# A conformer block on one core: two query blocks moved to an earlier place in attention, and a feed-forward block moved in front of the last query block

## The chip, the cores and the metric

The kernel runs on one core of one Trainium2 chip. The metric is the device time of one execution in microseconds (us). Run times are compared between kernels that ran on the same chip in the same rounds. In the profile, PE is TensorE's matmuls, PEld its weight loads, ACT is ScalarE, DVE is VectorE, POOL is GpSimd, SP is the DMA queue's engine.

## The reference, cut to what matters

```python
B, T, D, K = (2, 4000, 512, 3); F = 4 * D
h = _layernorm(x);  x1 = x + 0.5 * (_silu(h @ w_ff1_a) @ w_ff1_b)
h = _layernorm(x1); q, k, v = h @ w_q, h @ w_k, h @ w_v
p = _softmax(jnp.einsum('btd,bsd->bts', q, k) * scale)
x2 = x1 + jnp.einsum('bts,bsd->btd', p, v) @ w_o
# [...] then a gated convolution over time, a second feed-forward, a last layer norm
```

The kernel folds `w_q` and `w_k` into one matrix M, so one projection of the queries ("query block", four of them for a chunk) is all that stands before the scores.

## The kernel before: the parts concerned

Tokens are cut into 16 chunks of 508 (4 tiles of 127), 8 for each batch. Attention goes over the chunks of queries (`g`), and within each over 32 key tiles (`kt`). Four PSUM banks S take scores, query blocks and other things in turn; four banks Y collect the values of a chunk. The values of a key tile run four tiles behind its scores (`LAG`): `self.lags` is a queue of matmul groups that wait their turn, and `pop(n)` issues the next n of them. The "seam" below is the place where the last values of one chunk end and the first of the next begin.

```python
def q_group(self, b, qc, dc):                       # one query block: 4 matmuls, one copy
    s, sl = qc % 2, 1 if b or qc else 0             # sl: slot with the transposed rows
    ps, b_ps = self.sbank()
    for cc in range(DC):
        self.mm(out, self.M[:, cc, dc*128:(dc+1)*128], self.lnT[sl][:, :, cc, lo:lo + W // TPC], ...)
    # dc odd: VectorE copies the bank to qT[s]; dc even: ScalarE does

def attention(self, old, hook, done):
    LAG = 4
    for g in range(NCK):
        # [...]
        for kt in range(KT):
            # scores: 4 matmuls  ->  ScalarE: exp  ->  VectorE: acc += P
            # [...]
            self.lags.append(values)                # 4 matmuls into the Y banks
            if g == 0 and kt < LAG:
                self.pop({0: old // 2, 1: old - old // 2}.get(kt, 0))
            elif len(self.lags) > LAG:
                self.pop(1)
            if g + 1 < NCK and 7 <= kt < 7 + TPC:
                self.fetch_queries((g + 1) // TCB, (g + 1) % TCB, kt - 7)
            if g + 1 < NCK and kt in (14, 16, 18, 20):
                self.q_group((g + 1) // TCB, (g + 1) % TCB, (kt - 14) // 2)
            # [...]
            hook(g, kt)                             # from g = 2 on: a convolution block at kt 3

def copy_o(self, g):                                # when a chunk's last values are issued
    for dc in range(DC):                            # (simplified to the usual chunk)
        self.away("DVE" if dc % 2 else "ACT", self.OT[:, dc, lo:hi], self.Yb[dc][:, lo:hi], ...)

# between feed-forward and attention:
for dc in range(DC):
    self.q_group(0, 0, dc)                          # two feed-forward blocks are still pending
```

The last values of chunk `g` are issued at tile 3 of chunk `g + 1`; `copy_o` then empties the Y banks, and the first values of chunk `g + 1` at tile 4 want them again. Slot 1 of `lnT` shares its upper half with `sT`, the transposed sums of the chunk that just ended.

Of the kernel before, what the change touches and what calls it, by code (L numbers as in the profile page):

```python
# [16 lines left out]
TPC = 4  # L17
CHUNK = TPC * TILE
N = B * T
TCB = -(-T // CHUNK)  # L20
NCK = B * TCB
# [6 lines left out]
DC = D // 128  # L28
# [7 lines left out]
def width(c):  # L36

    return CHUNK if c % TCB < TCB - 1 else T - (TCB - 1) * CHUNK
# [214 lines left out]
class Conformer:  # L253
# [604 lines left out]
                                           reads=b_o[lo:hi], writes=[Buf("out")]))  # L858


    def q_group(self, b, qc, dc):

        s, sl = qc % 2, 1 if b or qc else 0
        ps, b_ps = self.sbank()
        W = width(qc)
        out = ps[:, 0:W].rearrange("p (t k) -> p t k", t=TPC)
        lo = self.query_at(qc, 0)[1]
        for cc in range(DC):
            self.mm(out, self.M[:, cc, dc * 128:(dc + 1) * 128], self.lnT[sl][:, :, cc, lo:lo + W // TPC],
                    cc == 0, cc == DC - 1, [self.b_M] + self.b_lnT[sl], b_ps)  # L870
        if dc % 2:
            self.S.op("DVE", lambda e: e.tensor_copy(self.qT[s][:, dc, 0:W], ps[:, 0:W]),  # L872
                      reads=[b_ps], writes=[self.b_qT[s][dc]])
        else:
            self.act(self.qT[s][:, dc, 0:W], ps[:, 0:W], AF.Copy, [b_ps], [self.b_qT[s][dc]])
# [6 lines left out]
        return qc * CHUNK + ti * n - lo, lo  # L882

    def fetch_queries(self, b, qc, ti):
        sl = 1 if b or qc else 0
        src, rd = self.keys_at(b, self.query_at(qc, ti)[0])
        self.transpose(self.lnT[sl][:, ti], src, rd, [self.b_lnT[sl][ti]])

# [35 lines left out]
    def attention(self, old, hook, done):  # L924
        S = self.S
        LAG = 4
        for g in range(NCK):
            b, qc = divmod(g, TCB)
            s, W = qc % 2, width(g)
            if self.any_score:  # L930
                if qc == 0:
                    self.pop(len(self.lags))
                    if b:
                        for kt in range(KT):
                            self.key_tile(1, kt)
                self.row_max(qc)
            for kt in range(KT):
                kc, kj = divmod(kt, TPC)
                ps, b_ps = self.sbank()
                p = self.nxt("Pa", self.NP - 1) if self.any_score else self.nxt("P", self.NP)  # L940
                for cc in range(DC):
                    self.mm(ps[:, 0:W], self.hT[kc][:, kj, cc, :], self.qT[s][:, cc, 0:W],
                            cc == 0, cc == DC - 1 and not self.any_score,
                            [self.b_hT[kc][kj], self.b_qT[s][cc]], b_ps)
                if self.any_score:
                    self.mm(ps[:, 0:W], self.one3, self.m3[:, 0:W], False, True,
                            [self.b_one3] + self.b_m3, b_ps)
                self.act(self.P[p][:, 0:W], ps[:, 0:W], AF.Exp, [b_ps], [self.b_P[p]], scale=SCALE)
                if kt == 0:
                    S.op("DVE", lambda e, p=p: e.tensor_copy(self.acc[s][:, 0:W], self.P[p][:, 0:W]),  # L950
                         reads=[self.b_P[p]], writes=[self.b_acc[s]])
                else:
                    n = REST if kt == KT - 1 else 128
                    acc = self.acc[s][0:n, 0:W]
                    S.op("DVE", lambda e, p=p, n=n, acc=acc: e.tensor_tensor(  # L955
                        out=acc, in0=acc, in1=self.P[p][0:n, 0:W], op=ALU.add),
                        reads=[self.b_P[p], self.b_acc[s]], writes=[self.b_acc[s]])

                if kt == KT - 1:
                    self.split_sums(g)  # L960
                    if g < NCK - 1:
                        self.sums_by_query(s)

                def values(kt=kt, p=p, g=g, W=W):
                    for dc in range(DC):

                        r = slice(dc * REST, (dc + 1) * REST) if kt == KT - 1 else slice(0, 128)
                        self.mm(self.Yb[dc][:, 0:W], self.h[kt][r, dc * 128:(dc + 1) * 128], self.P[p][r, 0:W],
                                kt == 0, kt == KT - 1, [self.b_h[kt], self.b_P[p]], self.b_Y[dc],
                                inc=kt == KT - 1 or dc == DC - 1,  # L970
                                **({"tile_position": (dc * REST, 0)} if kt == KT - 1 else {}))
                    if kt == KT - 1:
                        self.finish_queries(g, done)

                self.lags.append(values)
                if g == 0 and kt < LAG:
                    self.pop({0: old // 2, 1: old - old // 2}.get(kt, 0))
                elif len(self.lags) > LAG:
                    self.pop(1)
                if g + 1 < NCK and 7 <= kt < 7 + TPC:  # L980
                    self.fetch_queries((g + 1) // TCB, (g + 1) % TCB, kt - 7)
                if g + 1 < NCK and kt in (14, 16, 18, 20):
                    self.q_group((g + 1) // TCB, (g + 1) % TCB, (kt - 14) // 2)
                if not self.any_score and TCB - 1 <= g <= TCB:

                    at = (g - TCB + 1) * KT + kt
                    for k in range(KT):
                        if 6 + k * (2 * KT - 12) // KT == at:
                            self.key_tile(1, k)
                hook(g, kt)  # L990
                self.tick()
# [350 lines left out]
    def program(self, any_score):  # L1342
# [50 lines left out]
        old = 0  # L1393
        for c in range(NCK):
            ff1(c, old)
            old = len(self.lags)
        for dc in range(DC):
            self.q_group(0, 0, dc)

        tail = NCK - 2  # L1400
# [236 lines left out]
```

## Time and profile before

| | before |
|---|---|
| time, first three runs | 2042.21 us median (2041.98 to 2042.29) |
| span in the profile | 2037.6 us |
| TensorE busy | 100% |
| granted TensorE clock (share of full speed) | 0.999 |
| start to start, 508 columns | 215 ns median of 6,194 matmuls |
| stall at the last query block of chunk 0 (453 us) | 0.30 us |
| stall at the first seam of attention (516 us) | 0.90 us |

The stalls in this document are read from the starts of successive matmuls, less 215 ns each; the prediction says why the busy share does not show them. The list of TensorE's waits in the kernel before (columns: engine, line, waited for, total us, times, longest us) shows only a part of the seam:

```profile
PE s L512 <- DVE work L1326: 1.2, 1, 1.2
PE y L527 <- DVE work L644: 1.0, 2, 0.8
PE y L512 <- DVE work L559: 0.4, 1, 0.4
```

The first two lines lie in the first 9 us of the program. The third line is the seam: L559 is VectorE's copy of a Y bank. The list gives it 0.4 us, because a wait starts to count only when the drawn end of the last matmul is past, and a matmul is drawn longer than the distance to its successor; the starts give it 0.9 us.

### The profile page before, as it was taken

The numbers are of one execution on the slowest core, as the hardware profiler recorded it, in microseconds if no ns is written. First come the engines' busy times: TensorE is split into PE (matmuls) and PEld (weight loads), VectorE is DVE, ScalarE is ACT, GpSimd is POOL, SyncE is SP. The second block draws the span as 40 slices with busy tenths as digits, with TensorE's granted clock in tenths as the row PEclk, the third lists the DMA queues.
The fourth block names the chain that finished last, engine by engine and source line by source line (L and its number), as shares of the span: only waits on it lengthen the run. The fifth ranks groups of instructions, "written<-read, shape, count | busy, mean of one in ns | idle before, by whom it ended". The sixth has DMA issues, their size and how long they took to land.

```text
span 2037.6 us, 24579 instructions
## 1 busy us (share of the span) xinstructions
PE 2028.8 (100%) x9682; PEld 1030.0 (51%) x9682; DVE 1081.6 (53%) x2187; ACT 743.6 (36%) x1277; POOL 107.6 (5%) x235
## 2 busy tenths in 40 slices
PE   9999999999999999999999999999999999999999
PEld 5555555554444444445444444444455555555555
DVE  4234443334556667666766676667674444434434
ACT  3433333333333333333333333333345443443433
POOL 1000000000000000000000000000011000000000
PEclk9999999999999999999999999999999999999999
DMA  8122245420101111114421111111243111111111
GB/s 189 49 62 62 54 101 124 96 70 8 27 16 26 26 32 26 26 24 94 108 58 23 26 27 34 23 27 26 44 135 93 32 32 42 32 32 42 26 37 38
DMA packets 253121, 104.42 MB, mean 51 GB/s; under 512 B 193412, under 2 KB 252487, under 8 KB 252999
## 3 DMA queue, kind: packets, MB, share of 16 engines
q1 hardware_dynamic: 251793, 102.18, 21.6%
q8 instruction: 78, 1.28, 0.3%
q10 hardware_dynamic: 1206, 0.60, 0.1%
q14 instruction: 44, 0.36, 0.1%
HBM read 33.77 MB, written 23.34 MB: 28 GB/s over the span
## 4 chain that ended last, share of the span: by engine, by line
PE 98%; ACT 1%; DVE 0%; DMA 0%; SPq 0%; issue 0%; ACTq 0%
PE s L512 56%; PE y L512 42%; ACT work L562 0%; DMA xt<-in_x_dram 0%; ACT keys L562 0%; SPq L574 0%; PE y L540 0%; DVE work L559 0%; ACT L562 0%; PE y L527 0%; DVE work L872 0%; DVE work L955 0%; DVE wff L1208 0%; DVE wff L1095 0%; ACT wff L562 0%
## 5 line engine op out<-in xcount | busy, mean ns | idle before, releaser
L562 ACT ACTIVATE work<-s 128x508 bf16<-128x508 f32 (+3 forms) x1060 | 621.6, 587 | 1212.6 <-PE s L512 1208.1
L512 PE MATMUL s<-work,wff 128*128 128x508 bf16 (+4 forms) x2640 | 628.3, 369 | 0.6 <-DVE work L559 0.2
L512 PE MATMUL s<-work,keys 128*128 128x508 bf16 (+1 forms) x2048 | 516.8, 374 | 0.1
L512 PE MATMUL y<-work,keys 128*128 128x508 bf16 (+2 forms) x2048 | 504.2, 373 | 0.4 <-DVE work L559 0.4
L512 PE MATMUL y<-wff,work 128*127 128x512 bf16 (+1 forms) x2000 | 501.4, 378 | 0.0
L955 DVE TENSOR_TENSOR work<-work 128x508 f32<-128x508 f32 (+2 forms) x496 | 334.4, 674 | 283.1 <-ACT work L562 282.1
L512 PEld LDWEIGHTS s<-work,wff 128*128 128x128 bf16 x2640 | 252.5, 98 | 276.9 <-issue 4.7
L512 PEld LDWEIGHTS y<-wff,work 128*127 128x127 bf16 x2000 | 274.4, 137 | 170.8
L512 PEld LDWEIGHTS s<-work,keys 128*128 128x128 bf16 x2048 | 199.5, 98 | 231.9 <-issue 0.6
L512 PEld LDWEIGHTS y<-work,keys 128*128 128x128 bf16 (+1 forms) x2048 | 193.5, 97 | 234.0 <-issue 6.2
L758 DVE SCALAR_TENSOR_TENSOR xt<-y,xt 127x512 bf16<-127x512 f32 x125 | 77.7, 683 | 364.6 <-PE y L512 364.6
L624 DVE BATCH_NORM_STATS2 work<-xt 127x6 f32<-127x512 bf16 x311 | 195.3, 676 | 4.9 <-DMA xt<-in_x_dram 4.8
L512 PE MATMUL s<-work 128*127 128x512 bf16 (+4 forms) x775 | 195.8, 377 | 1.2 <-DVE work L1326 1.2
L631 POOL TENSOR_TENSOR work<-work 127x4 f32<-127x4 f32 (+1 forms) x76 | 76.5, 1007 | 1128.1 <-DVE work L629 1128.1
L512 PEld LDWEIGHTS s<-work 128*127 128x127 bf16 (+2 forms) x775 | 94.7, 124 | 74.9 <-issue 2.7
L644 DVE TENSOR_SCALAR work<-xt,work 127x512 bf16<-127x512 bf16 x309 | 111.5, 406 | 27.2 <-POOL work L631 23.2
L758 DVE SCALAR_TENSOR_TENSOR xt<-s,xt 127x512 bf16<-127x512 f32 x55 | 38.0, 691 | 148.7 <-PE s L512 148.7
L758 DVE SCALAR_TENSOR_TENSOR xt<-s,work,xt 127x512 bf16<-127x512 f32 x64 | 48.0, 750 | 30.9 <-PE s L512 30.3
L1106 DVE SCALAR_TENSOR_TENSOR wff<-wff,s 128x508 bf16<-128x508 f32 (+1 forms) x57 | 38.7, 679 | 41.7 <-PE s L512 41.5
L562 ACT ACTIVATE wff<-s 128x508 f32<-128x508 f32 (+1 forms) x67 | 39.5, 591 | 54.9 <-PE s L512 54.9
L562 ACT ACTIVATE work<-keys,work 128x508 bf16<-128x508 bf16 (+1 forms) x68 | 52.2, 775 | 0.1
L1187 POOL COPY wff<-wff 128x1 bf16<-128x1 bf16 x56 | 10.4, 187 | 638.1 <-DVE wff L1106 635.3
(92 smaller groups left out, 412.8 us busy)
## 6 DMA issues: line engine op xcount, KB each, us to landing
keys<-keysd SPq DMA_DIRECT2D x62, 128.0 KB, 2.3
keysd<-work SPq DMA_DIRECT2D x14, 448.0 KB, 3.2
out_dram<-work SPq DMA_DIRECT2D x14, 448.0 KB, 3.2
dcvd<-wff SPq DMA_DIRECT2D x48, 127.0 KB, 1.9
keys<-dcvd SPq DMA_DIRECT2D x12, 508.0 KB, 4.9
xt<-in_x_dram SPq DMA_DIRECT2D x13, 448.0 KB, 4.8
wff<-in_w_ff_a_dram SPq DMA_DIRECT2D x14, 256.0 KB, 5.7
work<-work SPq DMA_TRANSPOSE x208, 2.5
```

What stands on the lines that cost most here:

```text
L512: self.S.op("PE", lambda e: e.matmul(out, lhsT, rhs, start=start, stop=stop, **kw), reads=reads, writes=[bank], inc=stop if inc is None el ...
L562: return self.S.op("ACT", lambda e: e.activation(out, in_, func, **kw), reads=reads, writes=writes)
L624: self.S.op("DVE", lambda e: e.bn_stats(self.st[sl][:, ti, 0:6], x), reads=[b_x], writes=[self.b_st[sl][ti]])
L631: S.op("POOL", lambda e: e.tensor_tensor(out=self.rs[sl][:, 0:n], in0=self.mv[sl][:, 0:n, 1], in1=self.neghalf[0:TILE, 0:n], op=ALU.pow), ...
L644: self.S.op("DVE", lambda e: e.tensor_scalar(out, x, self.mv[sl][:, ti, 0:1], self.rs[sl][:, ti:ti + 1], ALU.subtract, ALU.mult), reads=[b ...
L758: self.S.op("DVE", lambda e: e.scalar_tensor_tensor(out=self.XT[g][rows], in0=ps[rows], scalar=scalar, in1=self.XT[g][rows], op0=ALU.mult, ...
L955: S.op("DVE", lambda e, p=p, n=n, acc=acc: e.tensor_tensor(out=acc, in0=acc, in1=self.P[p][0:n, 0:W], op=ALU.add), reads=[self.b_P[p], sel ...
L1106: self.S.op("DVE", lambda e: e.scalar_tensor_tensor(out=out, in0=th, scalar=1.0, in1=ps[:, 0:W], op0=ALU.add, op1=ALU.mult), reads=[b_ps, ...
L1187: S.op("POOL", lambda e: e.tensor_copy(self.G[gs][:, jj, 0:1], self.G[gp][:, jj, CHUNK:CHUNK + 1]), reads=[self.b_G[gp][jj]], writes=[self ...
```

## The change

The intent: fill two stalls with work that is waiting anyway. The queries of chunk 2 are fetched during chunk 0 into slot 0, and two of their four query blocks are made at tiles 3 and 4 of chunk 1, around the seam. One of the two pending feed-forward blocks goes in front of the last query block of chunk 0.

```diff
+    def query_slot(b, qc):
+        return 1 if b or qc == 1 or qc > 2 else 0
@@ q_group, and the same in fetch_queries
-        s, sl = qc % 2, 1 if b or qc else 0
+        s, sl = qc % 2, self.query_slot(b, qc)
@@ attention
-                if g + 1 < NCK and 7 <= kt < 7 + TPC:
+                if g + 1 < NCK and g != 1 and 7 <= kt < 7 + TPC:
                     self.fetch_queries((g + 1) // TCB, (g + 1) % TCB, kt - 7)
-                if g + 1 < NCK and kt in (14, 16, 18, 20):
-                    self.q_group((g + 1) // TCB, (g + 1) % TCB, (kt - 14) // 2)
+                if g == 0 and 24 <= kt < 24 + TPC:
+                    self.fetch_queries(0, 2, kt - 24)
+                if g + 1 < NCK and kt in ((3, 4, 14, 16) if g == 1 else (14, 16, 18, 20)):
+                    self.q_group((g + 1) // TCB, (g + 1) % TCB, (3, 4, 14, 16).index(kt) if g == 1 else (kt - 14) // 2)
@@ program
         for dc in range(DC):
+            if dc == DC - 1:
+                self.pop(1)
+                old -= 1
             self.q_group(0, 0, dc)
```

More of the change, by code (lines that the diff above doesn't have):

```diff
@@ L858, in store_out @@
                                            reads=b_o[lo:hi], writes=[Buf("out")]))
+    @staticmethod
+    def query_slot(b, qc):
+        return 1 if b or qc == 1 or qc > 2 else 0
     def q_group(self, b, qc, dc):
-        s, sl = qc % 2, 1 if b or qc else 0
+        s, sl = qc % 2, self.query_slot(b, qc)
         ps, b_ps = self.sbank()
@@ L884, in fetch_queries @@
     def fetch_queries(self, b, qc, ti):
-        sl = 1 if b or qc else 0
+        sl = self.query_slot(b, qc)
         src, rd = self.keys_at(b, self.query_at(qc, ti)[0])
```

## The prediction

> **What bounds the kernel now.** I began with the busy row and the clock row of the page, then the chain that ended last, then the list of waits of TensorE, and last the timeline around the two places that the diff touches.
>
> ```profile
> PE 2028.8 (100%) x9682; PEld 1030.0 (51%) x9682; DVE 1081.6 (53%) x2187; ACT 743.6 (36%) x1277; POOL 107.6 (5%) x235
> ...
> PEclk9999999999999999999999999999999999999999
> ...
> PE 98%; ACT 1%; DVE 0%; DMA 0%; SPq 0%; issue 0%; ACTq 0%
> ```
>
> The reader is to see one bound from end to end: TensorE at 100%, its clock row nine tenths or more in every slice, and 98% of the last chain on it. Busy time alone could hide gaps, because matmuls overlap. So I took the distance from one matmul's start to the next in the trace: the median is 215 ns for 508 columns and 216 ns for 512 (6,194 and 2,548 matmuls). A stretch of TensorE time is then worth its matmuls times 0.215 us, and anything beyond that is a stall. Only a stall can be won here: the change leaves the number of matmuls as it is.
>
> The first place is the last query block of chunk 0 (L512 with s<-work is a query block, s<-work,keys are scores), where feed-forward ends and attention starts. The timeline of all engines, columns start, duration, engine, line, operation, count, idle before:
>
> ```profile
> 452.79 0.53 PEld L512 LDWEIGHTS s<-work,keys 128*128 128x128 bf16 x3
> 452.95 1.28 ACT L562 ACT_TABLE_LOAD   x1
> 453.00 1.33 PE L512 MATMUL s<-work,keys 128*128 128x508 bf16 x4
> 453.20 0.69 DVE L872 CAST work<-s 128x508 bf16<-128x508 f32 x1 [1.04 <-PE s L512]
> 453.94 0.10 PEld L512 LDWEIGHTS s<-work,keys 128*128 128x128 bf16 x1 [0.63 <-DVE work L872]
> ```
>
> Four score matmuls take 1.33 us where they take 1.02 elsewhere. The fourth needs the last quarter of the queries, and its weight load waits for the VectorE copy of that quarter. The starts of the third and the fourth matmul are 0.512 us apart: a stall of 0.30 us.
>
> The second place is the seam between chunk 0 and chunk 1 of attention. The same view there:
>
> ```profile
> 515.67 0.39 PE L512 MATMUL y<-work,keys 32*128 32x508 bf16 x4
> ...
> 516.00 1.03 PE L512 MATMUL s<-work,keys 128*128 128x508 bf16 x4
> 516.33 1.08 ACT L562 ACTIVATE work<-y 128x508 bf16<-128x508 f32 x2
> ...
> 516.97 0.39 PE L512 MATMUL y<-work,keys 128*128 128x508 bf16 x1
> 517.07 1.27 DVE L559 CAST work<-y 128x508 bf16<-128x508 f32 x2
> ...
> 517.80 0.98 PE L512 MATMUL y<-work,keys 128*128 128x508 bf16 x3 [0.45 <-DVE work L559]
> ...
> 518.62 0.59 PE L512 MATMUL s<-work,keys 128*128 128x508 bf16 x2
> ```
>
> The values of chunk 0 end in four small matmuls at 515.67 into the four y banks. Then come the scores of key tile 4, and then the first values of chunk 1, which want the same banks. ScalarE and VectorE empty two banks each, and TensorE waits. From 515.997 (first score) to 518.619 (next scores) are 2.62 us for 8 matmuls worth 8 x 0.215 = 1.72: a stall of **0.90 us**. At the later seams, such as the one at 581 us, eight matmuls of a convolution block stand in this place and no stall shows; the first seam has no such block, because that work follows its chunk by one or two.
>
> **What the Trainium skill says.** "Perfetto Trace Analysis", section "Identifying the Most-Contended Engine", says that matmul busy time is a poor measure because matmuls are pipelined. The trace agrees: it gives 370 to 380 ns to a matmul whose successor starts 215 ns later. "TensorE: Matmul & The Clock Gate", section "Step-by-step: what each phase is for", says that only weight loads are pulled ahead and the matmuls stay in program order. That fits both stalls: independent matmuls stand behind the waiting one and do not pass it. "TensorEngine Tiling (Array Packing)", section "Key Properties", says that changing the tiling mode drains the engine. Around the four 32-row matmuls the starts lose 95 and 101 ns at the seams; the change leaves these.
>
> **Part one: the queries of chunk 2.** Before, their transposed rows went into slot 1, whose upper half is also used by the transposed sums of the chunk just ended; the queue shows the last two of these fetches starting only after 520 us. The diff puts them into slot 0, free since the query blocks of chunk 0 (453 us), and asks for them during chunk 0, so they lie ready long before 515. It then moves two of the four query blocks from key tiles 18 and 20 of chunk 1 to tiles 3 and 4 (the other two stay at 14 and 16). Nothing is added: 8 matmuls change place.
>
> The compiled order of the changed kernel shows where they land: the first block directly after the four small matmuls, before the scores of tile 4, and the second only after the four value matmuls that wait. So only the first, 4 x 0.215 = 0.86 us, lies in front of the stall. Worked through with the releases of before:
> - first query block 515.997 to 516.87; scores of tile 4 to 517.73;
> - value matmul 1 at 517.73; its bank was free at 516.97 before. No wait.
> - value matmul 2 at 517.94; it could start at 517.80 before. No wait.
> - value matmul 3 at 518.16; no wait.
> - value matmul 4 at 518.37; it could start at 518.394 before: about 0.02 us is left.
> - scores of tile 5 at 518.62, the same time as before, now with a query block done.
>
> The gain is that block, **0.86 us**, out of 0.90. For the releases to stay put, ScalarE must take its two bank copies before the new query copy, and the code does emit them first. VectorE's copy for the second block comes after its bank copies too. The second block is neutral: 0.86 us earlier here, 0.86 us fewer later, where there was no stall to fill.
>
> **Part two: the feed-forward block.** Three matmuls (0.65 us) move from behind the first scores to a place in front of the last query block. The stall, though, lies behind that block: from its last matmul (start 452.784) through the copy (453.200, 0.69 us) to the fourth score (453.944) is 1.16 us, in which three score matmuls run. In the changed order the query block is still followed at once by those scores, so the same 1.16 us with the same three matmuls remain. The moved block fills a time in which TensorE was not waiting. I choose a gain of **0.00 us**. Behind the query block it would have covered the 0.30.
>
> Sum: 2042.21 - 0.86 - 0.00 = **2041.35 us**.
>
> **Rivals.**
> 1. *The early block gets in the way of the releases.* ScalarE's new copy, about 0.59 us, could delay the exponentials, or VectorE's, 0.69 us, the sum of 1.21 us at 518.85. For it: VectorE is the engine whose copies end last. Against: both copies come behind the bank copies, and the engines are 36% and 53% busy. If the second bank copy of VectorE slipped by one instruction, 0.6 us of the gain would go: about 2041.9.
> 2. *Slot 0 becomes a new wait.* The layer norm of chunk 0 writes its transposes there, at 545.63 before, and the last query block reading the slot is at tile 16, at 543.53 before for the second block of that time. I expect both some 0.86 us later, the block still ahead; and the convolution reads the slot only at 556. A wait here would stay off TensorE. Effect 0.
> 3. *The feed-forward block does cover the last copy.* For it: the diff seems meant so. Then up to 0.30 us more: 2041.05. Against: the order.
> 4. *All is lost in the noise.* The three runs before lie within 0.31 us, so 0.86 should show, unless another chip or occasion shifts the base.
>
> **Range and chances.** 2041.35, with 0.30 below from rival 3 and 0.55 above from rival 1, widened by the spread of the runs: 2040.8 to 2042.0. Two per cent would be 40.8 us. All stalls of more than 40 ns in the trace, the start included, come to 11 us, so faster by over 2% is impossible by this path: 0.003. Slower would need a new wait in a place I have not found: 0.007. Within 2%: 0.99.
>
> **What would show it.** In the changed trace: a group of query matmuls between the 32-row matmuls and the scores at 516 us; value matmuls spaced 215 ns apart but for at most some 0.05 us before the fourth; no group left at tiles 18 and 20; scores of tile 5 starting within 0.1 us of the old instant, 518.62. At 453 to 455 us, the last score matmul still waiting 0.3 us for VectorE. Span shorter by 0.8 to 0.9. A time above 2042.0, a value matmul waiting for VectorE by over 0.3 us, or no stall at 454 would prove me wrong.

## The result, and the profile after

The changed kernel took **2041.36 us** (median of 4 runs, 2041.07 to 2041.77); the kernel before took 2042.25 us (median of 4 runs, 2041.98 to 2042.35). The medians differ by 0.89 us. Ratios are the mean time of one kernel's fast runs over that of the other's of the same rounds, so not quite the ratio of the medians: 0.9996, with a 95% interval of 0.9979 to 1.0013. The interval is far too wide for an effect of 0.04%, and the effect is therefore read from the traces.

The page of the changed kernel, the same rows as the prediction shows of before (busy time, clock, shares of the last chain):

```profile
PE 2028.4 (100%) x9682; PEld 1030.0 (51%) x9682; DVE 1081.6 (53%) x2187; ACT 743.7 (37%) x1277; POOL 107.6 (5%) x235
...
PEclk9999999999999999999999999999999999999999
...
PE 99%; ACT 1%; DVE 0%; DMA 0%; SPq 0%; issue 0%
```

The same 9,682 matmuls, the same bound and the same clock: nothing was removed, only moved. The timeline of the changed kernel around the last query block of chunk 0:

```profile
452.27 0.81 PE L512 MATMUL y<-wff,work 128*127 128x512 bf16 x3
...
452.91 1.03 PE L512 MATMUL s<-work 128*128 128x508 bf16 x4
453.08 1.28 ACT L562 ACT_TABLE_LOAD   x1
...
453.78 2.19 PE L512 MATMUL s<-work,keys 128*128 128x508 bf16 x8
453.98 0.69 DVE L876 CAST work<-s 128x508 bf16<-128x508 f32 x1 [1.69 <-PE s L512]
454.72 0.76 PEld L512 LDWEIGHTS s<-work,keys 128*128 128x128 bf16 x5 [0.62 <-DVE work L876]
```

The feed-forward block (first line) now stands ahead of the last query block, and the weight load of the fourth score still waits for VectorE's copy (last line), as it did before. The stall is 0.30 us by the starts in both traces.

And around the first seam:

```profile
515.80 0.39 PE L512 MATMUL y<-work,keys 32*128 32x508 bf16 x4
...
516.13 1.04 PE L512 MATMUL s<-work 128*128 128x508 bf16 x4
516.46 1.07 ACT L562 ACTIVATE work<-y 128x508 bf16<-128x508 f32 x2
...
517.00 1.02 PE L512 MATMUL s<-work,keys 128*128 128x508 bf16 x4
517.20 1.27 DVE L559 CAST work<-y 128x508 bf16<-128x508 f32 x2
...
517.86 1.05 PE L512 MATMUL y<-work,keys 128*128 128x508 bf16 x4
...
518.75 1.03 PE L512 MATMUL s<-work 128*128 128x508 bf16 x4
```

A query block (second line, s<-work) stands where TensorE waited. The copies of the banks by ScalarE and VectorE begin where they did, 0.66 and 1.40 us after the four small matmuls, and the four value matmuls run in one group of 1.05 us instead of two groups with a hole between them. The matmul starts leave 0.06 us of stall, where the same reckoning gave 0.91 before: the 20 matmuls behind the four small ones, less 20 times 0.2147 us. The wait on L559 by a value matmul is gone from the list of TensorE's waits, whose longest lines are now:

```profile
PE y L527 <- DVE work L644: 1.2, 2, 0.9
PE s L512 <- DVE work L1333: 1.2, 1, 1.2
PE y L540 <- ACT work L562: 0.2, 1, 0.2
```

**A measure finer than the run time.** The whole time carries the start and the end of the program. From the span's start to TensorE's hundredth matmul, the traces range from 13.19 to 13.85 us; from the last matmul to the end, from 5.08 to 6.72 us (5.08 and 6.46 us in two runs of the kernel before). So each trace was also reduced to TensorE's time from its hundredth (counted from zero) to its last matmul: 2019.27 us before, 2018.30 us after. Of this difference of 0.97 us, 0.12 belongs to another stall, at 961 us, that was 0.29 us in one trace and 0.18 in the other. The repeats below show that it comes and goes. Without it: 2018.98 and 2018.13 us, **0.85 us**. Larger stalls were left alone: read from the starts in the same way, six of 0.24 to 0.41 us, 1.9 us together, stand between 1496 and 1548 us of the kernel before, and the changed kernel has the same six.

### The profile page after: what moved, and what is told of

It is laid out like the page before. It is cut to its first block, busy times and chain, and to the rows that moved or that the text cites. A ratio compares the mean times of both kernels' runs of the same rounds, so it can differ in the third digit from the quotient of the medians.

```text
span 2037.2 us, 24581 instructions
## 1 busy us (share of the span) xinstructions
PE 2028.4 (100%) x9682; PEld 1030.0 (51%) x9682; DVE 1081.6 (53%) x2187; ACT 743.7 (37%) x1277; POOL 107.6 (5%) x235
## 3 DMA queue, kind: packets, MB, share of 16 engines
q8 instruction: 78, 1.28, 0.3%
## 4 chain that ended last, share of the span: by engine, by line
PE 99%; ACT 1%; DVE 0%; DMA 0%; SPq 0%; issue 0%
PE s L512 56%; PE y L512 42%; ACT work L562 0%; DMA xt<-in_x_dram 0%; ACT keys L562 0%; SPq L574 0%; PE y L540 0%; ACT L562 0%; PE y L527 0%; DVE work L559 0%; DVE work L876 0%; DVE wff L1215 0%; DVE wff L1102 0%; ACT wff L562 0%; ACT xt L562 0%
```

## The experiments

The theory: a stall is worth only the matmuls that stand, in TensorE's order, behind what starts the wait and in front of the matmul that waits. By it the whole gain is the first query block; the second one and the feed-forward block fill nothing. The rivals: the feed-forward block does cover the query copy; both query blocks share the gain; the early fetch is the gain; the seam waits for something other than the bank copies.

All kernels gave correct results. "TensorE" is the time from the hundredth to the last matmul without the stall at 961 us; "453" and "516" are the two stalls. These last four columns come from one trace for each kernel and compare it with the first trace of the kernel before, while e1, e2, e3 and e8 ran on chip 9, the other runs and the repeats on chip 15 (for the first two traces no chip is on record). What such a comparison is worth is seen from r_before (chip 15) and e2 (chip 9, no gain expected), which differ from that first trace by 0.02 and 0.01 us.

| run | time, median us | ratio to before | TensorE us | against before | 453 us | 516 us |
|---|---|---|---|---|---|---|
| before | 2042.25 | | 2018.98 | | 0.30 | 0.91 |
| after | 2041.36 | 0.9996 | 2018.13 | -0.85 | 0.30 | 0.06 |
| e1_queries_only | 2041.65 | 0.9996 | 2018.13 | -0.85 | 0.30 | 0.06 |
| e2_block_only | 2042.19 | 0.9999 | 2018.99 | +0.01 | 0.30 | 0.91 |
| e3_block_behind | 2041.14 | 0.9993 | 2017.82 | -1.16 | 0.00 | 0.06 |
| e8_copies_first | 2041.54 | 0.9994 | 2018.27 | -0.71 | 0.30 | 0.18 |
| e5_first_only | 2041.33 | 0.9993 | 2018.13 | -0.85 | 0.30 | 0.05 |
| e6_behind_wait | 2042.23 | 0.9997 | 2018.98 | 0.00 | 0.30 | 0.91 |
| e7_fetch_only | 2042.42 | 0.9998 | 2019.00 | +0.02 | 0.30 | 0.91 |
| e9_both_covered | 2041.06 | 0.9992 | 2017.79 | -1.19 | 0.00 | 0.02 |

The kernel before took 2042.53 us (median of 9 runs, 2042.05 to 2043.43) beside e1, e2, e3 and e8, and 2042.50 us (9 runs, 2041.70 to 2044.32) beside the other four. Every ratio's interval reaches both sides of 1, so the verdicts rest on the last four columns. The differences of the run medians agree with them within 0.35 us. Taken by run medians, e2, e3, e6, e8 and e9 miss the change from before that was expected of them by 0.1 to 0.25 us, each towards a larger gain; the runs of the kernel before beside them spread over 1.4 and 2.6 us.

**e1_queries_only** takes the feed-forward part out of the changed kernel.

```diff
-            if dc == DC - 1:
-                self.pop(1)
-                old -= 1
             self.q_group(0, 0, dc)
```

> The changed kernel without the feed-forward part: the queries of chunk 2 move, the feed-forward block stays behind the first scores. Theory (all of the gain is the query block in the seam): 0.85 to 0.9 us faster than before, time as the changed kernel's within 0.15 us, the seam's stall at most 0.06 us, the 0.30 us stall at 453 us unchanged. Rival (the feed-forward block covers the last query copy): 0.3 us slower than the changed kernel.

TensorE's time is the changed kernel's to the hundredth. The feed-forward part is worth nothing.

**e2_block_only** puts that part alone into the kernel before (the same lines, added).

> The kernel before with the feed-forward part alone. Theory: no gain, within 0.15 us of before, the last score matmul still starts 1.16 us after the last query matmul (stall 0.30 us), the seam's stall 0.87 to 0.90 us as before. Rival (the block covers the copy): the stall at 453 us gone, 0.3 us faster.

No gain: +0.01 us on TensorE. Its timeline, the query block, the scores, the copy and the waiting weight load:

```profile
452.75 1.03 PE L512 MATMUL s<-work 128*128 128x508 bf16 x4
...
453.61 2.19 PE L512 MATMUL s<-work,keys 128*128 128x508 bf16 x8
453.81 0.69 DVE L872 CAST work<-s 128x508 bf16<-128x508 f32 x1 [1.69 <-PE s L512]
454.55 0.76 PEld L512 LDWEIGHTS s<-work,keys 128*128 128x128 bf16 x5 [0.62 <-DVE work L872]
```

VectorE was idle for 1.69 us before its copy (1.04 us in the kernel before): the moved block only made VectorE wait longer for the query block, and the weight load's wait for VectorE stayed as it was.

**e3_block_behind** moves the block, in the changed kernel, from the front of the last query block to its back.

```diff
-            if dc == DC - 1:
-                self.pop(1)
-                old -= 1
             self.q_group(0, 0, dc)
+        self.pop(1)
+        old -= 1
```

> The changed kernel with its feed-forward block behind the last query block instead of in front of it. Theory: three more matmuls (0.65 us) stand in the 1.16 us between the last query matmul and the fourth score, so the stall of 0.30 us goes to 0: 0.30 us faster than the changed kernel, 1.15 to 1.2 us faster than before. Rival (the stall is not the copy's but that of the start of attention, for instance the exponential's table load): the stall stays or moves to the next scores, no gain over the changed kernel.

The stall is gone, and TensorE is 0.31 us faster than in the changed kernel. Its timeline there:

```profile
452.97 1.28 ACT L562 ACT_TABLE_LOAD   x1
453.03 0.81 PE L512 MATMUL y<-wff,work 128*127 128x512 bf16 x3
453.23 0.69 DVE L876 CAST work<-s 128x508 bf16<-128x508 f32 x1 [1.04 <-PE s L512]
453.46 1.60 PEld L512 LDWEIGHTS s<-work,keys 128*128 128x128 bf16 x8
453.67 1.88 PE L512 MATMUL s<-work,keys 128*128 128x508 bf16 x8
```

The feed-forward block runs while VectorE copies; the eight scores take 1.88 us instead of 2.19, and no wait is noted on their weight loads. The table load of ScalarE is in the same place, so it was not what TensorE waited for.

**e8_copies_first** has no part of the change. In chunk 1 alone, VectorE's running sum of key tile 3 is issued after its bank copies.

```diff
+                    late = g == 1 and kt == LAG - 1
+                    if not late:
+                        add()                  # VectorE: acc += P, as before
 # [...]
                 elif len(self.lags) > LAG:
                     self.pop(1)                # issues the last values and the bank copies
+                if g == 1 and kt == LAG - 1:
+                    add()
```

> The kernel before, neither part of the change; only in chunk 1, VectorE's running sum of key tile 3 is issued after its two bank copies instead of before them. Theory (the seam waits for bank releases that stand behind that 0.69 us sum): the copies end some 0.7 us earlier, the stall of 0.87 us shrinks to 0.1 to 0.2 us, 0.7 to 0.8 us faster than before, without any matmul moved. Rival (the seam waits for something else, as the start of the values or the four 32-row matmuls): stall and time as before.

TensorE gains 0.71 us without one matmul moved; the stall falls to 0.18 us. The seam in this kernel:

```profile
515.90 0.39 PE L512 MATMUL y<-work,keys 32*128 32x508 bf16 x4
...
516.35 1.28 DVE L559 CAST work<-y 128x508 bf16<-128x508 f32 x2 [0.69 <-PE y L512]
516.55 1.07 ACT L562 ACTIVATE work<-y 128x508 bf16<-128x508 f32 x2
517.19 0.11 PEld L512 LDWEIGHTS y<-work,keys 128*128 128x128 bf16 x2 [0.43 <-ACT work L562]
517.20 1.09 PE L512 MATMUL y<-work,keys 128*128 128x508 bf16 x4
...
517.55 1.47 DVE L956 TENSOR_TENSOR work<-work 128x508 f32<-128x508 f32 x2
```

VectorE's copies begin 0.45 us after the small matmuls, not 1.40, and the sum comes behind them (last line). What is left of the wait names ScalarE (fourth line). So the cause of most of the stall is one sum of 0.69 us, with its own wait for an exponential (1.03 us idle before it in the kernel before), in VectorE's order ahead of the copies. The change covers this wait; e8 shortens it.

**e5_first_only** keeps the first query block at tile 3 and puts the others at tiles 12, 14 and 16. The edit is cut to the tiles; the line around them became a loop over the four blocks.

```diff
-  (3, 4, 14, 16)
+  (3, 12, 14, 16)
```

> The changed kernel with only the first query block at tile 3; the second at tile 12 (then 14 and 16 as in the change). Theory (the second block at tile 4 fills nothing): time as the changed kernel's within 0.15 us, seam stall at most 0.06 us. Rival (both blocks fill the seam): 0.3 to 0.45 us slower than the changed kernel.

It is the changed kernel's time on TensorE: the second early block adds nothing.

**e6_behind_wait** has `(4, 12, 14, 16)` in that place: one early block, at tile 4, behind the waiting values.

> The changed kernel with one query block in the seam, at tile 4 alone, which puts it behind the waiting value matmuls, (then tiles 12, 14, 16). Theory: no gain from the seam, stall 0.87 to 0.90 us as before, time as before within 0.15 us. Rival (a block anywhere near the seam helps): 0.85 us faster than before.

No gain at all. The seam in this kernel:

```profile
516.32 1.03 PE L512 MATMUL s<-work,keys 128*128 128x508 bf16 x4
...
517.29 0.39 PE L512 MATMUL y<-work,keys 128*128 128x508 bf16 x1
...
518.12 0.98 PE L512 MATMUL y<-work,keys 128*128 128x508 bf16 x3 [0.45 <-DVE work L559]
...
518.94 1.03 PE L512 MATMUL s<-work 128*128 128x508 bf16 x4
```

The query block (last line) starts 0.8 us after a value matmul that had waited; no wait of its own is noted. TensorE did not take it ahead of the waiting one.

**e7_fetch_only** has `(10, 12, 14, 16)`: the early fetch, and no block at the seam.

> The changed kernel with the early fetch into slot 0, but all four query blocks at tiles 10, 12, 14 and 16, none in the seam. Theory: the fetch itself is worth nothing; stall and time as before within 0.15 us. Rival (the freed slot or the shorter DMA queue is the gain): 0.5 us or more faster than before.

+0.02 us on TensorE: the early fetch by itself gains nothing. It is what lets a query block stand at the seam, since before the last two of these fetches started only at 520.14 and 521.37 us.

**e9_both_covered** is the version that the others point to: the block of e3, and `(3, 3, 14, 16)`, both early query blocks ahead of the waiting values.

> The version the experiments point to: feed-forward block behind the last query block, and both early query blocks at tile 3, in front of the waiting values. Theory: seam stall 0, stall at 453 us 0: 0.30 + 0.90 = 1.20 us faster than before, some 0.33 us faster than the changed kernel. Rival (the second block in front delays ScalarE's exponential or VectorE's copies and makes a new wait): no better than the changed kernel with the block behind.

TensorE is 1.19 us faster than before and 0.34 us faster than the changed kernel. The second block in front is worth the 0.03 us that were left. It is the fastest kernel on TensorE's time and by its median run time, 2041.06 us (five runs, 2040.71 to 2041.17), which lies below all nine runs of the kernel before on the same chip (lowest 2041.70).

**The repeats**, r_before and r_after, are one look each.

> The kernel before once more, for one look at the stall of 0.29 us that its first trace shows at 961 us (start of the convolution block, four query transposes behind key loads in the DMA queue), which was 0.18 us in the changed kernel's trace. Theory (it comes and goes from run to run, and has nothing to do with the change): it may be anything from 0 to 0.3 us here, while the stalls at 453 and 516 us repeat to 0.02 us. Rival (the change shortens it): again 0.29 us here.

> The changed kernel once more, for the same look. Theory: the stall at 961 us differs from the 0.18 us of the first trace or from the repeated kernel before without order, and TensorE's time from its hundredth to its last matmul, less that stall, is 0.85 us under that of the kernel before. Rival: 0.18 us again, and less than in the kernel before.

The stall at 961 us was 0.09 us in the repeat of before and none in that of after (0.29 and 0.18 in the first traces; 0.28 in e1; 0.04 in e9; none in e2, e3, e5, e6, e7 and e8). It differs between two runs of one kernel, so it says nothing of the change. It stands where a convolution block reads transposed rows that come by DMA. In the five traces with the stall the block's first matmul starts 0.24 to 0.25 us after the last of four transposes lands, in the other seven 0.25 to 0.60 us after. That fits a wait for this landing; no run changed the DMA to test it. Without it TensorE's time repeats to 0.02 us: 2019.00 and 2018.13 us. Their run times, 2042.93 and 2042.18 us, are single runs of unknown state.

## Why the prediction was right, point by point

- **The sum, 2041.35 us.** The run median is 2041.36 us. That it agrees to 0.01 us is luck, since the four runs spread over 0.70 us; what tests the sum is the 0.85 us on TensorE beside the 0.86 foreseen.
- **One bound, no matmul removed.** Right: the same 9,682 matmuls at the same clock.
- **Part one, 0.86 us by the first query block.** Right: 0.85 us (after, e1 and e5). The second block was called neutral: e5 and e6 show it.
- **The releases stay put.** Right: the bank copies begin 0.66 and 1.40 us after the small matmuls in both traces. Left over are 0.06 us, not 0.02: 23 ns before the fourth value matmul, as reckoned, some 10 ns twice where one kind of matmul follows another, and a few ns elsewhere.
- **"Scores of tile 5 at 518.62".** A slip, and one of its signs that did not come: in the changed kernel the second query block starts there (518.75) and those scores come behind it, at 519.61. The prediction had itself put the second block directly behind the value matmuls. The gain does not hang on it.
- **"Span shorter by 0.8 to 0.9".** This sign did not come either: the profiled spans are 2037.6 and 2037.2 us. The end of the program, from the last matmul on, took 5.08 us in one trace and 5.59 in the other, so the span was too coarse a sign.
- **Part two, 0.00 us.** Right: e1 and e2 show no effect, and e3 shows the 0.30 us to be had on the other side of the query block.
- **Rival 1, new copies delaying the releases.** It did not happen. VectorE's sum of 1.21 us moved from 518.85 to 520.42, which reached nobody on TensorE.
- **Rival 2, slot 0.** The transposes of the layer norm start at 546.68, behind the last query block at 544.53; no wait, as expected. Not foreseen was that the early fetch starts only at 472 us, behind a store of keys in the same DMA queue; there are still 44 us left to the seam.
- **Rival 3, the feed-forward block covering the copy.** Refuted by e2.
- **Rival 4, noise.** It was nearly true of the run times: the medians show the gain, the intervals do not. In the first comparison all four runs of the changed kernel (at most 2041.77) lie below all four of the kernel before (at least 2041.98), but the later runs of the kernel before spread from 2041.70 to 2044.32 us.
- **"The trace agrees", of "Perfetto Trace Analysis".** The cited section says that pipelined TensorE instructions look smaller in the trace. Here they are drawn longer than their distance (370 to 380 against 215 ns), so the trace agrees on the overlap and not on the look.

## What to carry to other kernels

In this kernel one engine works in strict order and is busy throughout. What a moved block was worth could be counted from the order and the length of the stall: it filled a stall only between the instruction whose result is awaited and the instruction that waits, and only as far as the stall went (the second block in front, in e9, was worth the 0.03 us left). A block a few places away, in front or behind, was worth nothing, as the feed-forward block and the second query block show. Ask also what makes the wait long: here an unrelated sum in front of two copies on VectorE made most of it, and turning their order gained 0.71 of the 0.91 us without touching TensorE.

## What the Trainium skill lacked or had wrong

- "TensorE: Matmul & The Clock Gate", section "Back-to-back issue gap", gives some 131 ns for each matmul of 512 columns as the sustained rate of load and matmul pairs. Here 2,548 matmuls of 512 columns, each with its own weight load, start 216 ns apart (median), 215 ns at 508 columns. The page's other formula, N/2.4 + 2.5, fits: it gives 215.8 and 214.2 ns.
- "ScalarE: Activation LUTs", section "What ACT_TABLE_LOAD costs", gives 1.28 us for the load and 1.38 us of drain. The load took 1.28 us here; but in the kernel before it began 0.02 us after the end of ScalarE's copy before it (452.95 against 452.93), and the exponential began 0.14 us after its end (454.37 against 454.23). So no such drain stood on either side of it.
- "TensorEngine Tiling (Array Packing)", section "Key Properties", says that a change of tiling mode drains the engine, without a figure. Around the four 32-row matmuls at the seams the starts lose 95 and 101 ns; that the drain is what takes them was not tested.
- No page read gives, as one figure, the time from a matmul to the consumer of its bank and back. Here the copy of a query block begins 0.416 us after the start of its last matmul, takes 0.69 us on VectorE, and the weight load that waits for it starts 0.05 us after its end: 1.16 us. Three other matmuls in between left 0.30 us of it open, six (e3) none; by the distance of 215 ns five would do, which is an estimate.
